# A new opening for a Fourier mixer with an ELU layer pair: the filter straight into SBUF, the first unit's layer products plain, the weight conversion rearranged

## The chip, the core and the metric

One core of a Trainium2 chip. The kernel is one program; its time is the device time of one execution in microseconds (us), the median of the runs shown. TensorE (PE) does the matrix products, VectorE (DVE) and ScalarE (ACT) the work on elements, GpSimd (POOL) mostly issues DMA transfers, SyncE (SP) issues nearly all others. Each engine works through its own instructions in their order.

## The reference

Two blocks, one after the other. The first filters along the sequence: a real Fourier transform over 3008 positions, a product with a complex filter, and the inverse transform. The second is a layer pair with ELU between.

```python
# x (8, 3008, 256) f32; filt_r, filt_i (1505, 256) f32
X = np.fft.rfft(x, axis=1)
Y = X * (filt_r + 1j * filt_i)[None]
y = np.fft.irfft(Y, n=3008, axis=1).astype(np.float32)
# y -> (24064, 256); w_in (256, 2048), w_out (2048, 256), both float64
h = y @ w_in
g = np.where(h > 0, h, np.exp(np.minimum(h, 0.0)) - 1.0)
out = (g @ w_out).astype(np.float32)
```

The layer weights arrive as 64-bit floats: 4.2 MB each. The kernel reads them as pairs of 32-bit words and makes 32-bit floats of them itself.

## The kernel before

**Fourier part.** 3008 = 47 x 64. The transform over 64 is a product with a table (`tf`/`ta`, PE, "psa"), the transform over 47 a second one (`gf`/`fb`), the filter a complex product, and the way back mirrors it (`gr`/`gi`, then `tn`/`tw`, "psn"). The 32 frequencies of the 64-transform are worked in eight groups of four.

The first batch (b = 0) has code of its own, inside the `boot` pool. `x_load_first` loads x in six chunks on SP; `a_first` multiplies each chunk as it comes and ACT lays the results into `zt` (two of the four `zt` tiles live in the not yet filled weights `w_in[3]`, `w_out[3]`); `t_first` transposes group g on PE; `b_first` does the 47-transform and `products`, four DVE instructions with the filter tile `ff[:, g]`; `bi_first` goes back and ACT copies the result into one of two `t3f` buffers; `y_write_first` writes it to DRAM scratch `yds[0]`. In the loop over g (L900) group g's forward part stands beside group g-2's way back. After the loop `y_read` brings the first unit's rows from scratch, seven products called `warm` keep PE at work meanwhile, and `n_unit(0, 0)` makes the layer's input y.

The filter goes two steps for the first batch: `f_arrange` (L785) writes it into DRAM scratch `fd` in the order of the groups, 28 transfers on POOL, half of them reading with a negative row step; `f_read_first` (L319) reads `ff` from `fd`, 16 transfers on POOL. `f_pairs` (L804) makes the layout `fp` that the other seven batches read, from `fd`, on SP, in quads 1 to 4.

**Weights.** Sixteen blocks k = 0 to 15; k = 4q + j, where q is the quarter of the hidden width and j = 0, 1 are halves of `w_in[q]`, j = 2, 3 of `w_out[q]`. `w_fetch` loads the 64-bit words (512 KB), `w_split` (DVE, two instructions) takes mantissa and exponent bits apart, `w_float` (ACT, four instructions) makes floats of the low word, of the mantissa, and of the exponent in two steps, `w_join` (DVE) puts the sign on, adds low word and mantissa, multiplies with the exponent's value into place. `w_sums` (DVE, four sums) makes the extra combinations that the layer's seven products need. Blocks 0 to 11 are done before the layer starts, 12 to 15 in quads 0 to 2.

**Layer part.** A unit is (b, m): 8 batches, six units of up to 512 tokens. Per unit and quarter q, one quad, items in the order b, m, q. Both layers are 2 x 2 blocks multiplied with seven products instead of eight (`up_steps`, `down_steps`; `COMBO` names the weight combination). Each product is two matmuls of 224 or 256 columns, four records in the trace: so 28 matmuls per quad. An up product lands in one of four PSUM banks "psM" (`bank`, `banks`, first in, first out); ACT copies some of them, DVE adds, ACT does the two steps of ELU (Relu, then Exp), DVE the last one (max) and the sums for the seven down products, which gather in the banks po0 to po3. The down products of a quad run beside the up products of the next one.

**Order.** Everything is in one hand-written order: `at(quad, place, fn)` puts a piece into a plan, and the loop at the end (L1022) takes up and down steps by turns ("UUDUDDU", then "DUUDUDD", or with another start where a quad is in `opens`) and calls the plan's pieces at places 2 and 3 (within the first string), 0 (between the strings) and 1 (after the second). Quad i = 4 is the first of unit (0, 1). In the first quads the next batch's first stage stands too: `x_unit` (DVE, two instructions each) for chunks 0, 1 at quad 2, 2, 3 at quad 3, 4, 5 at quad 4, and `a_unit`, which takes all four banks, after them; `z_write` and the first `z_read` go to SP, `b_unit` comes after quad 6.

SP's transfers use eight semaphores in turn, so each waits for the one eight before it.

Of the kernel before, what the change touches and what calls it, by code (L numbers as in the profile page):

```python
# [26 lines left out]
P = 128  # L27
# [14 lines left out]
def _make_tables():  # L42
# [78 lines left out]
    tw = np.ascontiguousarray(tn[:, 0:8].reshape(4, K2, 8, 2, 2, 32).transpose(1, 0, 2, 4, 3, 5)).reshape(P, 8, P)  # L121
# [12 lines left out]
def kernel(  # L134
# [48 lines left out]
    fd = fdp.tile([NG, 2, 48, 2, 2, D], FP32, name="fd")  # L183
# [105 lines left out]
    def t_first(g):  # L289

        t = t2s[0, g] = t4p.tile([P, 4, D], FP32, tag="t4", name="tf") if g % 4 > 1 else t2[:, g % 4]
        for j in range(2):
            i = j + 2 * (g % 2 if g < 4 else 0)
            ps = psO.tile([P, 2, 256], FP32, tag="po%d" % i, name="po%d" % i)
            for u in range(2):
                k = 4 * g + 2 * j + u
                for dh in range(2):
                    nc.tensor.transpose(ps[0:ROWS, u, ts(dh, P)], zt[k // 16][dh][:, ts(k % 16, ROWS)], eye)  # L298
            nc.scalar.activation(out=t[0:ROWS, 2 * j:2 * j + 2, :], in_=ps[0:ROWS], func=AXT.Copy)
# [19 lines left out]
    def f_read_first(g, t):  # L319
        for a, r in enumerate((LO, HI)):  # L320
            nc.gpsimd.dma_start(t[r].rearrange("p c u d -> p (c u d)"), fd[g, a].rearrange("q c u d -> q (c u d)"))
# [12 lines left out]
    def products(re, im, f, sr, si, p, q):  # L334

        nc.vector.tensor_tensor(out=sr, in0=re, in1=f[:, 0], op=ALU.mult)
        nc.vector.tensor_tensor(out=si, in0=re, in1=f[:, 1], op=ALU.mult)
        nc.vector.scalar_tensor_tensor(out=p, in0=im, scalar=-1.0, in1=f[:, 1], op0=ALU.mult, op1=ALU.mult)
        nc.vector.tensor_tensor(out=q, in0=im, in1=f[:, 0], op=ALU.mult)
# [144 lines left out]
    def y_read(b, m, *parts):  # L484
        t = t4s[b, m] = t4p.tile([P, 4, D], FP32, tag="t4", name="t4")
        for k in parts or (slice(0, K2),):
            if whole(b, m):
                r = slice(4 * k.start, 4 * k.stop)
                nc.sync.dma_start(t[r], yds[b].rearrange("k (p i) d -> (k p) i d", p=4)[r, 4 * m:4 * m + 4, :])
                continue  # L490
            for r in range(2):
                o = 64 * r
                nc.sync.dma_start(t[o + 2 * k.start:o + 2 * k.stop].rearrange("q i d -> q (i d)"),
                                  yds[b][k.start + r:k.stop:2].rearrange("k (p i) d -> k p (i d)", p=4)
                                  [:, :, 4 * m * D:4 * m * D + 4 * D])
# [5 lines left out]
    def n_whole(b, m):  # L501
# [10 lines left out]
        b11, b12, b21, b22 = rows  # L512
        t = yp.tile([P, 2, 256], FP32, tag="yb", name="yb")[:, :, 0:h]
# [38 lines left out]

    COMBO = {1: 0, 2: 2, 3: 6, 4: 3, 5: 4, 6: 5, 7: 1}
# [5 lines left out]
    def up_steps(b, m, q):  # L559

        h = half(m)
# [82 lines left out]
    def down_steps(b, m, q):  # L644
        h = half(m)
# [67 lines left out]
    def w_fetch(k, queue=nc.gpsimd):  # L713
        q, j = divmod(k, 4)

        if k in (3, 4, 14, 15):
            wd = t2[:, k % 11 - 3].rearrange("p u d -> p (u d)")
        elif k == 10:
            wd = t1p.tile([P, XC, D], FP32, tag="t1", name="wd").rearrange("p u d -> p (u d)")
        elif k in (6, 7, 8, 9):  # L720
            wd = xp.tile([P, 2, 2, D], FP32, tag="xc", name="wd").rearrange("p k u d -> p (k u d)")
        else:
            wd = fbufs[{5: 0, 11: 0, 12: 1, 13: 2}.get(k, k)].rearrange("p c u d -> p (c u d)")
# [14 lines left out]
    def w_split(k):  # L738
        m, e, f, l = wts[k] = wtmp[{9: 2, 10: 1, 11: 0, 12: 3, 13: 4, 15: 5}.get(k, k % 2)]
# [4 lines left out]
    def w_float(k, *parts):  # L744
        m, e, f, l = wts[k]
        ef = e.bitcast(FP32)
        steps = ((l, wds[k][:, :, 0], AXT.Identity, 2.0 ** -52, 0.0), (f, m, AXT.Identity, 2.0 ** -20, 1.0),
                 (ef, e, AXT.Relu, -8.0, edges[:, 0:1]), (e, ef, AXT.Relu, -1.0, edges[:, 1:2]))
        for i in parts or range(4):
            o, x, func, scale, bias = steps[i]  # L750
            nc.scalar.activation(out=o, in_=x, func=func, scale=scale, bias=bias)

    def w_join(k, parts=(0, 1)):
        q, j = divmod(k, 4)
        m, e, f, l = wts[k]
        if 0 in parts:
            nc.vector.scalar_tensor_tensor(out=e, in0=wds.pop(k)[:, :, 1], scalar=0x80000000, in1=e,
# [319 lines left out]
```

## Time and profile before

| what | us |
|---|---|
| median of 3 runs | 2560.32 (2559.58 to 2561.1) |
| profiled execution, its own time | 2561.57 |
| its span | 2559.8 |
| PE busy | 2519.9 |
| DVE busy | 2067.4 |
| ACT busy | 1543.9 |

The span runs from the first to the last instruction of the profiled execution. Three stretches of 20 us in the opening, from the view that sums each engine's busy time in a window (columns: window, its length, busy us and instructions of PE, its weight loads, DVE, ACT and POOL, the granted PE clock, the DMA engines' share, GB/s):

```profile
40.00:60.00 20.00, 19.01 (x144) 13.38 (x148) 15.52 (x31) 14.95 (x31) 9.56 (x18) 0.91 1.00 285
80.00:100.00 20.00, 15.73 (x74) 12.07 (x73) 16.70 (x36) 16.66 (x31) 0.00 (x0) 1.00 0.96 252
100.00:120.00 20.00, 18.33 (x104) 17.98 (x103) 18.81 (x36) 14.33 (x26) 0.00 (x0) 1.00 0.32 95
```

A matmul's record is drawn out while it waits, so a busy PE is not a PE at full speed: 74 records between 80 and 100 us, against 120 in 20 us further on. From some 160 us on PE is busy without a gap.

### The profile page before, as it was taken

How to read it: one execution, taken by the hardware profiler on the slowest of the kernel's cores; microseconds unless marked ns; L12 is line 12 of the kernel's file. 1: busy time of each engine (PE TensorE's matmuls, PEld its weight loads, DVE VectorE, ACT ScalarE, POOL GpSimd, SP SyncE). 2: the span in 40 equal slices, each digit the busy share in tenths (PEclk: the TensorE clock that was granted, in tenths of full speed). 3: DMA queues.
4: the chain of work that ended last, by engine and by line, in shares of the span. 5: the costliest groups of instructions: out<-in, count | busy, mean ns of one | idle time of the engine just before them, and what ended most of it. 6: DMA issues, size and time to landing. Idle time of an engine off the chain costs nothing.

```text
span 2559.8 us, 43989 instructions
## 1 busy us (share of the span) xinstructions
PE 2519.9 (98%) x16682; PEld 2162.6 (84%) x16682; DVE 2067.4 (81%) x3578; ACT 1543.9 (60%) x2715; POOL 159.5 (6%) x315
## 2 busy tenths in 40 slices
PE   6999999999999999999999999999999999999998
PEld 4788889888898888988889888888889888898887
DVE  6978887788878888688877888778897788876766
ACT  6766556655566555666566656566655655555554
POOL 5001000000000000000000000000100010000000
PEclk9999999999999999999999999999999999999999
DMA  9662213523233221433225231353213322110010
GB/s 282 183 186 67 59 44 78 131 63 71 48 99 98 69 66 40 127 81 74 51 51 143 66 77 36 77 123 80 66 38 84 87 63 63 38 44 18 20 27 17
DMA packets 229879, 200.56 MB, mean 78 GB/s; under 512 B 129398, under 2 KB 201990, under 8 KB 229668
## 3 DMA queue, kind: packets, MB, share of 16 engines
q1 hardware_dynamic: 214308, 166.86, 26.6%
q0 software_dynamic: 14000, 30.44, 4.2%
q8 instruction: 131, 2.15, 0.4%
q14 instruction: 80, 0.66, 0.1%
q10 hardware_dynamic: 1360, 0.46, 0.1%
HBM read 125.80 MB, written 78.12 MB: 80 GB/s over the span
## 4 chain that ended last, share of the span: by engine, by line
PE 96%; DMA 2%; DVE 1%; ACT 0%; issue 0%; SPq 0%; DVEq 0%; ACTq 0%
PE po L656 45%; PE phs L574 25%; PE phd L574 13%; PE pha L574 6%; PE psn L526 2%; PE psa L236 2%; PE pf L387 1%; PE pv L459 1%; DMA xc<-in_x_dram 1%; PE po L332 0%; DMA x<-in_x_dram 0%; PE po L298 0%; PE psr L332 0%; PE psa L279 0%; DVE g L582 0%
## 5 line engine op out<-in xcount | busy, mean ns | idle before, releaser
L656 PE MATMUL po<-g,wo 128*128 128x256 f32 (+1 forms) x5376 | 1317.7, 377 | 0.0
L656 PEld LDWEIGHTS po<-g,wo 128*128 128x128 f32 x5376 | 1010.7, 190 | 165.8 <-issue 49.6
L585 ACT ACTIVATE g<-phs 128x512 f32<-128x512 f32 (+1 forms) x576 | 338.8, 588 | 736.7 <-PE phs L574 735.3
L592 ACT ACTIVATE e<-e 128x512 f32<-128x512 f32 (+1 forms) x768 | 477.2, 621 | 24.4
L596 DVE SCALAR_TENSOR_TENSOR g<-e,g 128x512 f32<-128x512 f32 (+1 forms) x576 | 387.5, 673 | 13.7 <-ACT e L592 13.3
L582 DVE TENSOR_TENSOR g<-phd,g 128x512 f32<-128x512 f32 (+1 forms) x384 | 259.0, 674 | 165.1 <-ACT e L592 107.6
L574 PE MATMUL phs<-y,wi 128*128 128x256 f32 (+1 forms) x1536 | 387.6, 375 | 1.3 <-ACT y L509 1.3
L574 PE MATMUL phd<-y,wi 128*128 128x256 f32 (+1 forms) x1504 | 380.3, 375 | 0.0
L591 ACT ACTIVATE e<-g 128x512 f32<-128x512 f32 (+1 forms) x576 | 354.4, 615 | 34.3 <-DVE g L582 26.8
L574 PEld LDWEIGHTS phs<-y,wi 128*128 128x128 f32 x1536 | 291.4, 190 | 34.7 <-ACT y L509 1.5
L574 PEld LDWEIGHTS phd<-y,wi 128*128 128x128 f32 x1504 | 284.8, 190 | 35.1 <-DVE g L582 2.7
L596 DVE SCALAR_TENSOR_TENSOR g<-e,phs 128x512 f32<-128x512 f32 (+1 forms) x192 | 129.9, 677 | 115.2 <-ACT e L592 115.2
L574 PE MATMUL phs<-yt,wi 128*128 128x256 f32 (+1 forms) x768 | 193.9, 375 | 0.9 <-ACT g L585 0.9
L574 PE MATMUL phs<-yb,wi 128*128 128x256 f32 (+1 forms) x768 | 193.8, 375 | 0.6 <-ACT g L585 0.6
L574 PE MATMUL pha<-yb,wi 128*128 128x256 f32 (+1 forms) x736 | 185.9, 375 | 0.0
L591 ACT ACTIVATE e<-phs 128x512 f32<-128x512 f32 (+1 forms) x192 | 112.3, 585 | 111.9 <-PE phs L574 111.8
L582 DVE TENSOR_TENSOR g<-pha,g 128x512 f32<-128x512 f32 (+1 forms) x192 | 129.5, 674 | 44.8 <-PE pha L574 44.8
L574 PEld LDWEIGHTS phs<-yt,wi 128*128 128x128 f32 x768 | 145.7, 190 | 18.0 <-ACT g L585 1.5
L574 PEld LDWEIGHTS phs<-yb,wi 128*128 128x128 f32 x768 | 144.0, 190 | 19.3 <-ACT g L585 1.0
L326 POOL DMA_DIRECT2D fall<-fp x224 | 110.0, 499 | 721.9 <-DVE r L432 697.1
L574 PEld LDWEIGHTS pha<-yb,wi 128*128 128x128 f32 x736 | 139.8, 190 | 16.1
L633 DVE TENSOR_TENSOR g<-g,g 128x512 f32<-128x512 f32 (+1 forms) x192 | 130.7, 681 | 6.7
(166 smaller groups left out, 2063.3 us busy)
## 6 DMA issues: line engine op xcount, KB each, us to landing
yd<-t SPq DMA_DIRECT2D x127, 192.0 KB
t<-yd SPq DMA_DIRECT2D x92, 256.0 KB
z<-t SPq DMA_DIRECT2D x84, 256.0 KB
fall<-fp POOLq DMA_DIRECT2D x224, 96.0 KB, 2.9
t<-z SPq DMA_DIRECT2D x224, 96.0 KB
out_dram<-o SPq DMA_DIRECT2D x632, 32.0 KB
xc<-in_x_dram SPq DMA_DIRECT2D x84, 128.0 KB
xc<-in_x_dram SPq DMA_DIRECT2D x161, 64.0 KB
```

What stands on the lines that cost most here:

```text
L236: nc.tensor.matmul(p[o:o + 64, u, :], w[r, u, o:o + 64], src[r, u, :], start=True, stop=True)
L326: nc.gpsimd.dma_start(t[32 * a:32 * a + 24].rearrange("p c u d -> p (c u d)"), fp[g, a].rearrange("q c u d -> q (c u d)"))
L387: nc.tensor.matmul(pf[p][1][32 * a:32 * a + 32, js, :], fb[r, v, :], t2[r, js, a, :], start=True, stop=True, tile_position=(32 * p, 32 * a))
L526: nc.tensor.matmul(p[ts(c, 64), dh, ts(q, 64)], t[r, i - 4 * m, ds(dh * P + 64 * c, 64)], w[r, i - 4 * m, :], start=True, stop=True)
L574: nc.tensor.matmul(ps[:, a, 0:h], w_in[q][:, COMBO[n], a, :], y[n], start=start and a == 0, stop=True, skip_group_check=True)
L582: nc.vector.tensor_tensor(out=g[o], in0=i0, in1=i1, op=ALU.add)
L585: nc.scalar.activation(out=g[o], in_=i0, func=AXT.Copy)
L591: nc.scalar.activation(out=e, in_=src, func=AXT.Relu, scale=-1.0)
L592: nc.scalar.activation(out=e, in_=e, func=AXT.Exp, scale=-1.0)
L596: nc.vector.scalar_tensor_tensor(out=g[n], in0=es[n], scalar=1.0, in1=src, op0=ALU.subtract, op1=ALU.max)
L633: nc.vector.tensor_tensor(out=b12, in0=b22, in1=b12, op=ALU.subtract)
L656: nc.tensor.matmul(po[i][:, u, 0:h], w_out[q][:, COMBO[n], a, :], g[n][:, a, :], start=q == 0 and a == 0 and n in (1, 3, 6, 4), stop=True, ...
```

## The change

Five parts.

1. **Filter.** `f_arrange`, `fd` and the 16 reads are gone. `f_read_first(k, n)` loads rows k to k+n of the filter straight into `ff`, which has a new layout (real or imaginary, then 16 rows); once with 4 rows, once with 12. Per half and part: 24 partitions by one SP transfer; the mirrored rows, 16 partitions by SP and 7 by POOL. The SP ones stand behind x in the queue. The groups therefore hold other frequencies: two from the lower half, two from the upper (`t_first`, table `tw`), and later units read y's rows of the first batch by four transfers instead of two. `f_pairs` reads from the filter itself.
2. **First unit plain.** For (b, m) = (0, 0) each layer is eight products instead of seven (`plain_ups`, `plain_downs`), 32 matmuls per quad instead of 28. The DVE sums around them (adds, four sums after ELU, seven at the end) and the ACT copies between them go; four ELUs per quad stay.
3. **Conversion.** `w_float` has three ACT instructions instead of four; the mantissa's is now part of a DVE instruction in `w_join` that multiplies and adds. `w_float` writes the low word in place.
4. **When.** Blocks 0 to 3 before the last chunks of x are multiplied, one block in each of groups 3 to 8, block 10 begun after the loop; `w_join` of 10 to 15 and split and float of 11 to 15 in quads 0 to 2. No `w_sums` before quad 1; one to two of them at the ends or middles of quads 1 to 6. None of them on POOL.
5. **Queues.** Blocks 0 to 2 on POOL ahead of all else; all other blocks on SP: 3 behind chunk 3 of x, 4 to 8 behind the filter, 9 to 11 between y's writes, 12 to 15 behind y's read.

```diff
+    def f_read_first(k, n):
+        for c, src in enumerate((filt_r, filt_i)):
+            for a in range(2):
+                o, row, e = 64 * a, 16 * a + k, 1 if k == a == 0 else 0
+                nc.sync.dma_start(ff[o:o + 48:2, c, k:k + n].rearrange("q k d -> q (k d)"),
+                                  raw(src, row, [[64 * D, 24], [1, n * D]]))
+                for j, m, queue in ((0, 16, nc.sync), (16, 7, nc.gpsimd)):
+                    queue.dma_start(ff[o + 2 * j + 1:o + 2 * (j + m):2, c, k + e:k + n],
+                                    raw(src, 64 * (j + 1) - row - e, [[64 * D, m], [-D, n - e], [1, D]]))
...
     def f_pairs(c, u):
-        nc.sync.dma_start(dst[:, :, 0, :], src[:, 0:48:2, :])
+        nc.sync.dma_start(dst[:, :, 0, :], raw(src, u, [[2 * D, 2 * NG], [64 * D, 24], [1, D]]))
         g = 1 - u
-        nc.sync.dma_start(dst[g:, 1:24, 1, :], src[g:, 1:46:2, :])
+        nc.sync.dma_start(dst[g:, 1:24, 1, :].rearrange("g k d -> k g d"),
+                          raw(src, 64 - 2 * g - u, [[64 * D, 23], [-2 * D, 2 * NG - g], [1, D]]))
...
+    def plain_ups(b, m, q):
+        def step(i, j, k):
+            if k == 0:
+                held[i, j] = bank("php")
+            n, ps = held[i, j]
+            for a in range(2):
+                nc.tensor.matmul(ps[:, a, 0:h], w_in[q][:, 2 * k + i, a, :], rows[k][j],
+                                 start=k == a == 0, stop=True, skip_group_check=True)
+            if k == 1:
+                src = ps[:, :, 0:h]
+                e = ep.tile([P, 2, 256], FP32, tag="e", name="e")[:, :, 0:h]
+                nc.scalar.activation(out=e, in_=src, func=AXT.Relu, scale=-1.0)
+                nc.scalar.activation(out=e, in_=e, func=AXT.Exp, scale=-1.0)
+                nc.vector.scalar_tensor_tensor(out=g[i, j], in0=e, scalar=1.0, in1=src, op0=ALU.subtract, op1=ALU.max)
+                banks.append(held.pop((i, j))[0])
...
+    def w_float(k):
+        m, e = wts[k]
+        ef, l = e.bitcast(FP32), wds[k][:, :, 0]
+        steps = [(l.bitcast(FP32), l, AXT.Identity, 2.0 ** -52, 1.0),
+                 (ef, e, AXT.Relu, -8.0, edges[:, 0:1]), (e, ef, AXT.Relu, -1.0, edges[:, 1:2])]
...
+        nc.vector.scalar_tensor_tensor(out=f, in0=m, scalar=2.0 ** -20, in1=l, op0=ALU.mult, op1=ALU.add)
...
+                if 3 <= g < 9:
+                    if g > 3:
+                        w_join(g)
+                    w_split(g + 1)
+                    w_float(g + 1)
+                if 4 <= g < 7:
+                    w_fetch(g + 5)
...
+        for quad, place, fn, k in ((0, 2, w_join, 10), (0, 2, w_split, 11), (0, 2, w_float, 11),
+                                   (0, 0, w_join, 11), (0, 0, w_split, 12), (0, 0, w_float, 12),
+                                   (1, 2, w_join, 12), (1, 2, w_split, 13), (1, 2, w_float, 13),
+                                   (1, 0, w_join, 13), (1, 0, w_split, 14), (1, 0, w_float, 14), (1, 1, w_sums, 1),
+                                   (2, 2, w_join, 14), (2, 2, w_split, 15), (2, 2, w_float, 15), (2, 0, w_join, 15),
+                                   (2, 1, w_sums, 3), (2, 1, w_sums, 5), (3, 0, w_sums, 9), (3, 1, w_sums, 7),
+                                   (4, 1, w_sums, 13), (5, 1, w_sums, 11), (6, 1, w_sums, 15)):
```

More of the change, by code (lines that the diff above doesn't have):

```diff
@@ L772, in w_join, with w_sums @@
                 nc.vector.tensor_tensor(out=dst[:, i], in0=f[:, i], in1=e[:, i], op=ALU.mult)
-        if j % 2 == 1 and k < 7:
-            w_sums(k)
-    def w_sums(k, engine=nc.vector, parts=(0, 1, 2, 3)):
+    def w_sums(k, parts=(0, 1, 2, 3)):
         q, j = divmod(k, 4)
@@ L902 @@
                 if g < NG:
-                    b_first(g, ff[:, g], pqs[g % 2], back)
+                    b_first(g, [ff[:, c, 2 * g:2 * g + 2] for c in range(2)], pqs[g % 2], back)
                 else:
@@ L943 @@
         n_unit(0, 0)
-        n_sums(0, 0)
         PER = 24
```

242 lines of the change are left out of this document (111 added, 131 removed).

## The prediction

> **What bounds the kernel now.** I read the page first, then stretches of the opening, then the chain of waits, then TensorE, VectorE, ScalarE and the queues in order of time.
>
> ```profile
> span 2559.8 us, 43989 instructions
> PE 96%; DMA 2%; DVE 1%; ACT 0%; issue 0%; SPq 0%; DVEq 0%; ACTq 0%
> PE   6999999999999999999999999999999999999998
> ```
>
> TensorE (PE) ends the run with 96% of the chain, and only the first of the 40 slices (64 us each) shows it short of work. So the change counts in two ways: when TensorE reaches its unbroken run, and how much work it has. The chain and the order of time through the opening:
>
> ```profile
> 29.50 10.89 DMA x<-in_x_dram
> 40.53 3.63 PE psa L279 x16
> 49.39 0.69 DVE L336 TENSOR_TENSOR rq<-psr,ff 128x512 f32<-128x512 f32 x1 [3.71 <-PE psi L332]
> 77.63 0.59 ACT L365 ACTIVATE t<-po 128x512 f32<-128x512 f32 x1
> 84.71 2.02 PE L508 MATMUL psn<-tn,t 128*128 128x128 f32 x16 [1.45 <-DMA t<-yd]
> 88.01 1.02 PE L574 MATMUL phs<-y,wi 128*128 128x224 f32 x4 [1.28 <-ACT y L509]
> 136.37 1.02 PE L656 MATMUL po<-g,wo 128*128 128x224 f32 x4
> ```
>
> The last part of x lands at 40.4, the first filter product runs at 49.4, the last result of the eight frequency groups is copied at 78.2, the first layer product starts at 88.0, and the fifth quad at 136.4 (a quad is one quarter of the hidden width for one unit; from there on PE has no gap that matters). So the opening to the end of quad 3 is 136.4 us, in three stages: load (to 40), groups (49 to 78), first unit (88 to 136).
>
> ```profile
> 0.00:20.00 20.00, 3.89 (x17) 3.66 (x18) 14.00 (x26) 15.38 (x21) 11.92 (x26) 1.00 0.93 255
> 20.00:40.00 20.00, 12.11 (x64) 11.27 (x64) 9.15 (x20) 11.25 (x26) 8.72 (x16) 0.83 1.05 343
> ```
>
> The two columns at the end: DMA is busy throughout, at 255 and then 343 GB/s. The load stage is bound by bytes.
>
> **Load stage.** The copy of the filter into DRAM scratch (3.08 MB), the weights 4 to 6 and most of the filter no longer stand ahead of x. What must land up to x's end: x 3.08 MB, tables 1.57, weights 0 to 3 (4 x 512 KB) 2.10, the filter's 7-row parts that POOL issues early, 7/47 of 3.08 = 0.46; 7.2 MB. At the rates above: 5.1 MB by 20 us, then 2.1 MB / 343 GB/s = 6.1; x ends at 26, not 40.4. From x to the first product took 49.4 - 40.4 = 9.0, same instructions: 35. The rest of the filter and the small tables (2.9 MB, 8.6 us) land by 35 to 38; groups 0 and 1 need only the first 4 rows, group 2 starts at 40. The filter therefore costs nothing on this path; without that cover of 2 us, up to 5 us (bounds: 343 GB/s, and half that for 16-row and 24-row transfers, which no row shows filling the engines).
>
> **Group stage: VectorE becomes its bound.** Products cost 4 x 0.60 = 2.4 per group. A weight costs w_split 0.67 (76.91 to 77.58) and w_join 2.0:
>
> ```profile
> 100.31 0.68 DVE L757 SCALAR_TENSOR_TENSOR zq<-fall,zq 128x512 uint32<-128x512 uint32 x1
> 100.91 0.69 DVE L759 TENSOR_TENSOR zq<-zq 128x512 f32<-128x512 f32 x1
> 101.70 0.69 DVE L766 TENSOR_TENSOR wi<-zq 128x512 f32<-128x512 f32 x1
> 102.31 0.42 DVE L741 TENSOR_SCALAR t<-t 128x512 uint32<-128x512 uint32 x1
> ```
>
> (starts 100.31 to 102.31). The new fused multiply-add over integers isn't in the trace; nearest are L757's 0.60 between starts and 0.72 for the add with its wait. I take 0.72; the other end is worth under 1 us over the stage. ScalarE's float drops from four instructions to three; the one that writes in place is off the chain, since it waits for the DMA alone.
>
> Groups 0 to 2: 7.2. Group 3 with split 4: 3.1. Groups 4 to 7, each products, join, split: 4 x 5.07 = 20.3. Then no products hide ScalarE: two exponent steps 1.45, copy of group 6 1.07, join 8 and split 9 on VectorE meanwhile (30.6 + 1.4 + 2.0 + 0.7 = 34.7), exponents of 9 1.45, copy of group 7 1.07: 37.3. The result of group 0 is written behind weights 5 to 8 in SP's ring (2.25 MB with its table, about 8 us from 42, so 50), and group 2's copy into the same buffer waits for it from 46; ScalarE's float 5 slides, and join 5 by 0.8. End of stage: 35 + 37.3 + 0.8 = 73.1, against 78.2.
>
> From there to the first layer product was 88.0 - 78.2 = 9.8. Of it 1.7 was the copy of y waiting behind three conversions on ScalarE (its half was ready at 85.7, copied at 87.4); only conversion 10 is left there, under the 6.5 us of y's round trip. So 8.1, plus 0.8 for a colder PE, since its seven warming products now end 4 us before y comes: first layer product T = 82.0. **Gain so far 6.0.**
>
> **First unit: ScalarE and VectorE hand weights to and fro.** PE work: 32 + 24 products up to quad 4 at 0.755 (8 records take 1.51), 42.3; with 1.9 for the next unit's y and 2 x 1.9 for the next batch's first stage, 48.0. Before took 48.4 with 42.6 of work. Work alone would lose nothing. But before had only two floats (14, 15) left in it; after has five (11 to 15), six joins and five splits, written into one in-order queue with the ELUs:
>
> ELU's two steps 1.2, its VectorE max 0.55, join 2.0, split 0.67, the next float's exponents 1.45 (they need the split), hand-offs 0.15: 6.0 us before the next ELU. Those rows are these two, and L757 to L741 above:
>
> ```profile
> 92.83 0.57 ACT L591 ACTIVATE e<-g 128x448 f32<-128x448 f32 x1
> 93.43 0.58 ACT L592 ACTIVATE e<-e 128x448 f32<-128x448 f32 x1
> 111.97 1.47 ACT L751 ACTIVATE t<-t,edges 128x512 f32<-128x512 uint32 x2
> ```
>
> Quads 0 and 1 have two such cycles and two plain ELUs each, 2 x 6.0 + 2 x 1.2 = 14.4, while PE needs 6.0 and 12.1. A product's bank is free only after its max, and there are four. From T + 1.7: quad 0 to T + 16.1, quad 1 to T + 30.5, the copies of y to T + 31.7. PE waits about 3 us in quad 1, and 5 before quad 2. VectorE then: sums of weight 1 and of the next y 3.2 (T + 34.2), max, join 14, split 15 3.2, float 1.5, ELU 1.2 (T + 40.2), max, join 15, x_unit's four sums 0.55 + 2.0 + 2.65, two maxes 1.1: T + 46.5. Only then is the last of four banks free for a_unit, where PE has waited since T + 43. Its second half 1.0, quad 3's 16 products 12.1, the next a_unit 2.0: quad 4 starts at T + 61.6. Against 48.4: **13.2 lost.** The eighth down product in quad 4 adds 0.76. The weight sums that moved to quads 2 to 6 (1.6 each) lie under 12 to 15 us of PE in quads where VectorE has 3 to 5 us idle (139 to 160), and the first unit's output loses its seven adds; if not hidden, 1 to 2 us. y's four reads for two, on SP, lie 13 us ahead of need.
>
> Sum: -6.0 + 13.2 + 0.8 = +8.0. Profiled 2559.8 (2561.6 with what lies around the span, 1.3 above the median 2560.3): 2567.8 span, 2568.3 as a median; I say 2569 for a PE that cools in the 5 us wait (40.53 above: 16 records took 3.63 after 2.28 idle, against 2.02 after 1.41 at 24.98).
>
> **Rivals.**
> 1. *The waits in the first unit are hidden* (faster). If PE never waits for a bank, quad 4 starts at 82.0 + 48.0 = 130.0: -6.4 + 0.8, about 2555. For it: ScalarE has 8.9 us of work per quad, VectorE 8, under PE's 12.1. Against: the order above is fixed. It decides when the cycle is below (12.1 - 2.4) / 2 = 4.8 us. Chance 0.11. Half the waits: 2562, within 0.2% (5 us, about what a measurement here can tell). With milder openings 0.19.
> 2. *The opening gains nothing*: one queue doesn't draw 300 GB/s, or VectorE waits for the filter in each group. T = 88, 2575. For: all of the ten first filter transfers are under 100 KB. Against: SP issues eight before it waits for the first. 0.12.
> 3. *The pair filter goes through one engine.* f_pairs now writes odd rows as 23 rows of 15 or 16 KB-pieces; before as 15 or 16 rows of 23.
>
> ```profile
> DMA packets 337, 0.34 MB, mean 331 GB/s; under 512 B 1, under 2 KB 337, under 8 KB 337
> q1 hardware_dynamic: 337, 0.34, 99.5%
> ```
>
> This is 1.04 us of such a transfer in before: 16.6 engine-us for 337 packets, 49 ns each. If 23 rows sat on one engine, 345 and 368 packets would hold it 17 and 18 us, four times in quads 0 to 5, with SP's ring behind them. The last pair would land near T + 101, the next batch's z behind it, read at T + 104, where b_unit wants it at T + 102 (before it had 13 us of slack): +2, 2571; if each packet took 70 ns, z writes and y's read slip too: 2580 to 2600. Chance that it shows in the time: 0.18. The Trainium skill ("DMA: Bandwidth & Descriptors", "Why a DMA increments its semaphore by 16 and not by 1") gives a transfer as many engines as the largest number up to 16 that divides the slowest dimension of both sides: 15 or 16 for before's, which agrees with the engines full above, and one for 23 rows. By that rule this rival holds, at 2571.
>
> **How the numbers follow.** Forecast 0.40, its own range 2565 to 2574 (T 79 to 85, waits 10 to 15). Rival 3 0.18, rival 2 0.12, between 0.19, rival 1 0.11. Faster 0.11, same 0.19, slower 0.70. Range 2558 to 2584: it drops rival 1 and the jammed end of rival 3.
>
> **What would show it.** x's last psa near 26 to 30; first product near 35; first layer product near 82; in quads 0 to 2 ScalarE idle on VectorE's split, PE idle in three pieces of 2 to 5 us, quad 4 near 144; no f_pairs transfer holding SP. Wrong if quad 4 starts before 134, or if TensorE is broken after 160.

## The result, and the profile after

The changed kernel takes 2603.1 us (median of 4, 2598.86 to 2605.34) against 2560.71 of the kernel before beside it (2559.58 to 2561.97): ratio 1.0163, 95% interval 1.015 to 1.0175, so slower by 1.6%. The forecast was 2569, its range 2558 to 2584: too fast by 34. The profiled execution took 2598.86, the fastest of the four, with a span of 2597.1; the forecast's span was 2567.8, so 29.3 us are to be explained.

The page of the profile after, the lines that answer to the first fence of the prediction:

```profile
span 2597.1 us, 43965 instructions
PE 93%; DVE 2%; DMA 2%; SPq 1%; ACT 1%; issue 1%; DVEq 0%; ACTq 0%
PE   6798999999999999999999999999999999999998
```

PE still ends the run, but its share of the chain fell from 96 to 93%, SP's queue went from 0 to 1%, and two more of the 40 slices are thin. The loss lies in the first 260 us. The load stage, by windows (columns: window, length, busy us and instructions of PE, its loads, DVE, ACT and POOL, PE clock, DMA share, GB/s), then the order of time through the opening on PE, DVE and ACT:

```profile
0.00:20.00 20.00, 5.51 (x32) 5.18 (x32) 9.97 (x16) 13.29 (x19) 8.48 (x20) 1.00 0.94 228
20.00:40.00 20.00, 16.31 (x120) 14.93 (x124) 5.77 (x12) 11.48 (x28) 0.00 (x0) 0.83 0.89 210
```

```profile
31.76 2.02 PE L279 MATMUL psa<-t,x 128*128 128x128 f32 x16 [0.22 <-DMA x<-in_x_dram]
39.01 0.69 DVE L345 TENSOR_TENSOR rq<-psr,ff 128x512 f32<-128x512 f32 x1 [6.17 <-PE psi L340]
50.13 0.69 DVE L346 TENSOR_TENSOR rq<-psr,ff 128x512 f32<-128x512 f32 x1 [4.62 <-DMA ff<-in_filt_i_dram]
51.94 0.68 DVE L345 TENSOR_TENSOR rq<-psr,ff 128x512 f32<-128x512 f32 x1
81.41 0.59 ACT L374 ACTIVATE t<-po 128x512 f32<-128x512 f32 x1
88.13 3.24 PE L518 MATMUL psn<-tn,t 128*128 128x128 f32 x16 [2.29 <-DMA t<-yd]
91.16 1.21 PE L585 MATMUL php<-y,wi 128*128 128x224 f32 x3
153.63 1.02 PE L608 MATMUL po<-g,wo 128*128 128x224 f32 x4
```

x lands at 31.7 (before 40.4), the first filter product runs at 39.0 (49.4), group 2 waits for the filter until 50.1, group 3 begins at 51.9, the last group is copied at 82.0 (78.2), the layer begins at 91.2 (88.0), quad 4 at 153.6 (136.4). x came 8.7 us sooner and the layer 3.2 later. In the first unit PE has three clear gaps, each behind DVE's max of an ELU (L592):

```profile
101.14 1.02 PE L585 MATMUL php<-y,wi 128*128 128x224 f32 x4 [1.02 <-DVE g L592]
107.01 1.78 PE L585 MATMUL php<-y,wi 128*128 128x224 f32 x8 [1.82 <-DVE g L592]
120.77 3.36 PE L585 MATMUL php<-y,wi 128*128 128x224 f32 x8 [4.64 <-DVE g L592]
```

And behind quad 4 stands what the forecast left to a rival. Three of the four long stops of SP's queue, a window of the first of them, and the waits for z behind the third (from 150.9) and the last, with a window that shows PE's clock at 0.66. z is the first stage's results, written to scratch and read back.

```profile
108.89 12.29 SPq L870 DMA_DIRECT2D fp<-nil_t  x1
123.39 14.14 SPq L870 DMA_DIRECT2D fp<-nil_t  x1
179.67 12.37 SPq L870 DMA_DIRECT2D fp<-nil_t  x1
```

```profile
109.00:121.00 12.00, 6.61 (x40) 6.23 (x40) 6.42 (x13) 6.36 (x11) 0.00 (x0) 0.93 0.16 52
```

```profile
172.47 1.09 ACT L240 ACTIVATE t<-psa 128x512 f32<-128x512 f32 x2 [3.83 <-DMA z<-t]
174.10 2.08 PE L648 MATMUL phs<-yt,wi 128*128 128x256 f32 x4 [2.57 <-ACT g L659]
204.42 1.83 PE L396 MATMUL pf<-t,pairs 24*32 24x256 f32 x4 [6.41 <-DMA t<-z]
206.87 4.76 PE L396 MATMUL pf<-t,pairs 24*32 24x256 f32 x36 [0.62 <-DMA t<-z]
211.56 2.08 PE L732 MATMUL po<-g,wo 128*128 128x256 f32 x4
```

```profile
200.00:220.00 20.00, 14.93 (x71) 8.80 (x72) 8.37 (x15) 4.26 (x9) 1.95 (x4) 0.66 0.66 151
```

L870 is the 15 KB of zeros that `f_pairs` issues directly behind its 23-row transfer; the stop not shown, third in time, runs from 150.9 for 11.5 us. While SP stands there, the DMA engines are 0.16 busy; in the finer view from 110 to 120 us the rate soon falls to a flat 25 GB/s, 1 KB each 41 ns, and from 113 to 120 us the share is 0.07, about one engine of 16. 345 such packets are 14.1 us.

The first product of the second batch's way back ("pv") comes at 252.4 against 214.8; from there on the two kernels run alike. So the 37.6 us between the kernels at pv (37.3 in the whole span) are 3.2 to the layer, 14.1 in the first unit (62.5 for 48.4) and 20.3 from quad 4 to pv.

### The profile page after: what moved, and what is told of

It reads as the page before. It is cut to its first block, busy times and chain, and to the rows that moved or that the text cites. A ratio compares the mean times of both kernels' runs of the same rounds, so it can differ in the third digit from the quotient of the medians.

```text
span 2597.1 us, 43965 instructions
## 1 busy us (share of the span) xinstructions
PE 2543.7 (98%) x16714; PEld 2175.7 (84%) x16714; DVE 2049.0 (79%) x3543; ACT 1529.6 (59%) x2687; POOL 135.4 (5%) x272
## 4 chain that ended last, share of the span: by engine, by line
PE 93%; DVE 2%; DMA 2%; SPq 1%; ACT 1%; issue 1%; DVEq 0%; ACTq 0%
PE po L732 43%; PE phs L648 24%; PE phd L648 12%; PE pha L648 6%; PE psn L539 2%; PE pf L396 1%; PE psa L236 1%; PE pv L468 1%; DMA t<-tf_t 1%; PE php L585 1%; PE po L608 1%; SPq L781 0%; DMA z<-t 0%; DMA t<-yd 0%; DMA ff<-in_filt_i_dram 0%
## 5 line engine op out<-in xcount | busy, mean ns | idle before, releaser
L732 PE MATMUL po<-g,wo 128*128 128x256 f32 (+1 forms) x5264 | 1294.3, 378 | 0.0
L732 PEld LDWEIGHTS po<-g,wo 128*128 128x128 f32 x5264 | 990.8, 190 | 165.8 <-issue 49.0
L659 ACT ACTIVATE g<-phs 128x512 f32<-128x512 f32 (+1 forms) x564 | 332.3, 589 | 735.8 <-PE phs L648 734.4
L666 ACT ACTIVATE e<-e 128x512 f32<-128x512 f32 (+1 forms) x752 | 468.0, 622 | 23.9
L670 DVE SCALAR_TENSOR_TENSOR g<-e,g 128x512 f32<-128x512 f32 (+1 forms) x564 | 379.8, 673 | 13.4 <-ACT e L666 13.1
L656 DVE TENSOR_TENSOR g<-phd,g 128x512 f32<-128x512 f32 (+1 forms) x376 | 253.7, 675 | 166.7 <-ACT e L666 108.3
L648 PE MATMUL phs<-y,wi 128*128 128x256 f32 (+1 forms) x1504 | 380.8, 376 | 0.0
L665 ACT ACTIVATE e<-g 128x512 f32<-128x512 f32 (+1 forms) x564 | 347.5, 616 | 32.0 <-DVE g L656 27.2
L648 PEld LDWEIGHTS phs<-y,wi 128*128 128x128 f32 x1504 | 286.2, 190 | 33.3
L648 PEld LDWEIGHTS phs<-yt,wi 128*128 128x128 f32 x752 | 143.2, 191 | 19.5 <-ACT g L659 3.0
## 6 DMA issues: line engine op xcount, KB each, us to landing
yd<-t SPq DMA_DIRECT2D x127, 192.0 KB
```

The source lines that it names most:

```text
L648: nc.tensor.matmul(ps[:, a, 0:h], w_in[q][:, COMBO[n], a, :], y[n], start=start and a == 0, stop=True, skip_group_check=True)
L656: nc.vector.tensor_tensor(out=g[o], in0=i0, in1=i1, op=ALU.add)
L659: nc.scalar.activation(out=g[o], in_=i0, func=AXT.Copy)
L665: nc.scalar.activation(out=e, in_=src, func=AXT.Relu, scale=-1.0)
L666: nc.scalar.activation(out=e, in_=e, func=AXT.Exp, scale=-1.0)
L670: nc.vector.scalar_tensor_tensor(out=g[n], in0=es[n], scalar=1.0, in1=src, op0=ALU.subtract, op1=ALU.max)
```

## The experiments

Each took 3 or 5 rounds beside the kernel before, whose median was 2560.6 to 2563.1. The moments below are those of the profiled executions. x's end is that of its last "psa" product on PE; it lies between 33.8 and 39.3 in executions whose opening is the same up to there, so the columns count from one moment to the next.

| kernel | us | ratio (95%) | x's end | layer, behind x | 3rd a_unit, behind layer | pv, behind it |
|---|---|---|---|---|---|---|
| before | 2560.7 | | 44.1 | 43.9 | 59.9 | 66.9 |
| after | 2603.1 | 1.0163 (1.015-1.0175) | 33.8 | 57.4 | 74.7 | 86.5 |
| e1_pairs16 | 2584.1 | 1.0084 (1.0067-1.0101) | 38.7 | 57.7 | 75.5 | 68.2 |
| e2_before23 | 2592.3 | 1.0119 (1.0104-1.0134) | 42.7 | 46.3 | 61.6 | 93.6 |
| e3_split_first | 2571.0 | 1.004 (1.0025-1.0055) | 39.3 | 56.8 | 64.1 | 68.3 |
| e4_filter_once | 2599.2 | 1.015 (1.0135-1.0165) | 37.5 | 72.1 | 75.0 | 68.3 |
| e5_before_newconv | 2559.8 | 0.9994 (0.9985-1.0003) | 41.8 | 42.1 | 60.0 | 67.0 |
| e6_pitch61 | 2571.7 | 1.0044 (1.003-1.0058) | 34.5 | 58.1 | 64.3 | 68.2 |
| e7_convert_early | 2572.9 | 1.0041 (1.0027-1.0054) | 38.2 | 57.1 | 62.7 | 68.2 |
| e9_two_queues | 2583.2 | 1.0084 (1.007-1.0098) | 46.2 | 58.0 | 64.7 | 68.2 |
| e10_first_piece_only | 2570.9 | 1.0037 (1.0022-1.0051) | 35.5 | 58.5 | 65.0 | 68.2 |
| e11_weights_between | 2576.7 | 1.0063 (1.0048-1.0078) | 37.1 | 58.0 | 64.0 | 68.2 |
| e12_rows_upward | 2574.3 | 1.0055 (1.004-1.007) | 35.7 | 57.8 | 65.1 | 68.2 |
| e13_copies_first | 2571.5 | 1.0035 (1.0021-1.0049) | 38.5 | 52.9 | 67.0 | 68.2 |
| e14_convert_in_gap | 2568.1 | 1.0028 (1.0017-1.004) | 39.0 | 52.5 | 64.6 | 68.2 |
| e15_first_unit_28 | 2574.1 | 1.0053 (1.0039-1.0067) | 34.5 | 50.5 | 75.3 | 67.0 |

### SP's stops: e1 and e2

e1, the kernel after with the 23 odd rows in two transfers:

```diff
-        nc.sync.dma_start(dst[g:, 1:24, 1, :].rearrange("g k d -> k g d"),
-                          raw(src, 64 - 2 * g - u, [[64 * D, 23], [-2 * D, 2 * NG - g], [1, D]]))
+        for j, m in ((0, 16), (16, 7)):
+            nc.sync.dma_start(dst[g:, 1 + j:1 + j + m, 1, :].rearrange("g k d -> k g d"),
+                              raw(src, 64 * (j + 1) - 2 * g - u, [[64 * D, m], [-2 * D, 2 * NG - g], [1, D]]))
```

> The changed kernel with one edit: the odd rows of the pair filter go as 16 and 7 rows instead of 23. Theory A (a transfer of 23 rows sits on one DMA engine, SP is held 12 to 14 us behind each of the four, and the next batch's z is late): SP shows no hold over 2 us there, quads 4 to 8 lose nothing, 2603 falls by some 20 us to 2583 (2579 to 2587). Rival B (the loss after quad 4 comes from VectorE's moved sums and conversions, the transfers only stand beside it): at or above 2598.

2584.1: 19.0 less, with one transfer more in each `f_pairs`. pv comes 68.2 behind the third a_unit instead of 86.5, and no issue of `f_pairs` holds SP for more than 1.2 us. PE's only gap from 150 to 245 us is one of 1.1, and the `pf` products, 7.1 us from first to last in after, take 1.6. e2 gives the kernel before the same shape:

```diff
-        nc.sync.dma_start(dst[g:, 1:24, 1, :], src[g:, 1:46:2, :])
+        nc.sync.dma_start(dst[g:, 1:24, 1, :].rearrange("g k d -> k g d"),
+                          src[g:, 1:46:2, :].rearrange("g k d -> k g d"))
```

> The kernel before with one edit: the odd rows of the pair filter, still read from the scratch copy, go as 23 rows of 15 or 16 instead of 15 or 16 rows of 23; same bytes. Theory A: SP is held 12 to 14 us four times from 100 us on, and PE waits for z or y's rows behind it: slower by 5 to 20 us, 2566 to 2581. Rival B: 2560 to 2562.

30.9 us slower (2592.3 against 2561.4), more than expected; the same four rows are there:

```profile
101.84 13.08 SPq L811 DMA_DIRECT2D fp<-nil_t  x1
117.27 14.43 SPq L811 DMA_DIRECT2D fp<-nil_t  x1
```

So it is the transfer's outermost 23, and what else has changed is not needed for it. PE waits longer here than in after: 11.2 us behind ACT at 167.4 and 7.2 for z at 198.5.

### The first unit: e3 and e7

e3 is e1 with another order in quads 0 to 2: split and float of the next block ahead of the join of the last.

```diff
-        for quad, place, fn, k in ((0, 2, w_join, 10), (0, 2, w_split, 11), (0, 2, w_float, 11),
+        for quad, place, fn, k in ((0, 2, w_split, 11), (0, 2, w_float, 11), (0, 2, w_join, 10),
...
```

> e1_pairs16 with one more edit: in quads 0 to 2 w_split and w_float of the next weight block stand ahead of w_join of the last one, so that ScalarE's float no longer waits for the join. Theory C (ScalarE and VectorE hand a block to and fro in cycles of 6 us, five times, and PE waits for banks): the cycle falls to 4 us, the first unit from first layer product to quad 4 from 62.5 to 52 to 55 us, 7 to 10 us faster than e1_pairs16. Rival D (the first unit is long because of its 56 products, the next batch's first stage and the four banks): within 2 us of e1_pairs16.

13.1 us less than e1, more than the 7 to 10 expected; the third a_unit comes 64.1 behind the layer for 75.5. Of e1's gaps of 1.0, 1.8 and 4.7 us on PE, one of 1.1 is left. The hand-over between DVE and ACT was most of the loss (before has 59.9), by its order alone: no work was taken away. e7 takes blocks 10 and 11 out of the unit as well:

```diff
+            w_split(10); w_float(10); w_join(9); w_split(11); w_float(11); w_join(10); w_join(11)
-            w_join(9); w_split(10); w_float(10)
...
```

> e3_split_first with the weight blocks 10 and 11 converted before the first layer product, where VectorE and ScalarE stand idle for some 9 us while y goes to memory and back, and only blocks 12 to 15 inside quads 0 to 2. VectorE's work there is two joins of 2.0 and a split of 0.8 more, which fits. Theory C (ping-pong of conversion and layer in the first unit is what is left of its loss): the first x block's transforms of quad 1, which come 33.8 us behind the first layer product in e3 and 32.9 in before, come 31 to 33 behind it, the layer starts within 1 us of e3's 96, and the time is 2567 to 2570 (e3 2571.0). Rival D: it only moves: the layer starts 2 or more us later, or the unit keeps its length because PE's banks were not waiting for these blocks; time within 1.5 us of 2571.

1.4 us less in the unit (62.7), and 2572.9 (2567.89 to 2573.6): not to be told from e3.

### The opening: the filter

e4 is e1 with the filter in one piece, `for k, n in ((0, 16),)` in place of `((0, 4), (4, 12))`.

> e1_pairs16 with one more edit: the filter's 16 rows in one go, 10 SP transfers instead of 18. Theory E (SP's 0.65 to 0.9 us per issue bounds the filter's loading): first filter product later by 2 to 5 us, but group 2 no longer waits 4.6 us in the middle of its products, and the layer starts 2 to 4 us earlier: 2 to 4 us faster than e1_pairs16. Rival F (the engines bound it: 24 rows on few engines, short packets): between 1 us faster and 3 us slower.

Both theories missed: 15.1 us more. The layer comes 72.1 behind x. With no early piece, PE has nothing to do for 5.8 us, and its clock falls:

```profile
51.55 1.97 PE L340 MATMUL psr<-tf,once 48*64 48x512 f32 x2 [5.83 <-DVE rq L346]
```

```profile
46.00:48.00 2.00, 0.00 (x0) 0.00 (x0) 0.00 (x0) 0.47 (x1) 0.00 (x0) 1.00 0.91 151
56.00:58.00 2.00, 2.00 (x15) 1.22 (x11) 0.69 (x1) 0.00 (x0) 0.00 (x0) 0.50 0.21 78
66.00:68.00 2.00, 2.00 (x13) 0.39 (x6) 0.24 (x1) 0.17 (x1) 0.00 (x0) 0.50 0.00 0
```

From 51.6 to 70 us PE's records leave no gap, at half its clock; its 48x512 products take 1.06 us instead of 0.59. The filter was there at 50.8, hardly another time than in after (50.1), though SP was through with its issues 2 us sooner. That speaks against SP's issues as what sets the landing.

Then what does? From 42 to 50 us all engines are busy at some 200 GB/s, and at 390 once the weights follow. e6 and e12 try two causes, e6 with `61 * D` for `64 * D` as the filter's row distance, e12 with `[D, n - e]` for `[-D, n - e]`, starting at the other end.

> e3_split_first with the first batch's filter read at rows 61 KB apart instead of 64 KB: the same transfers, sizes and queues, but other rows of the filter, so the first batch is multiplied by wrong filter values. In the opening of the kernel after the change the cores' 16 engines are all busy from 42 to 50 us and move only 200 GB/s, and 390 GB/s as soon as the weights follow at 50; the filter's 12 KB packets take 863 ns each, where a 4 KB packet of the weights takes 160 to 170. Theory P: it is the 64 KB between the rows that all engines read at once. Then at 61 KB the 12 KB packets take 500 to 650 ns, the stretch from 42 to 50 shows 280 GB/s or more, group 2's product waits 2 to 4 us less for its data, and the time is 2567 to 2570 (e3 2571.0). Rival Q: short runs into few partitions are slow whatever the pitch: 12 KB packets stay above 800 ns, 190 to 215 GB/s, time within 2 us of 2571.

> e3_split_first with the odd filter rows of the opening read upward through memory instead of downward: the same rows and bytes in the reverse order, so that each partition gets them in the wrong order and the first batch is multiplied by wrong values. Downward each row is a packet of 1 KB; upward 12 rows are one run. Theory O (the 200 GB/s from 42 to 50 us come from the 1 KB packets, of which some 2450 lie between 24 and 62 us): the 1 KB packets fall by about 1000, the stretch shows 260 GB/s or more, group 2's data lands 2 or more us earlier, time 2567 to 2569 against 2571. Rival P: the 12 KB packets go on taking 800 ns and more and the stretch stays below 220 GB/s: time 2570 to 2573, and the cause lies elsewhere.

Neither. In e6 the 12 KB packets take 872 ns on average (840 in e3); the windows:

```profile
44.00:48.00 4.00, 4.00 (x31) 2.45 (x29) 1.26 (x2) 1.27 (x3) 0.00 (x0) 1.00 1.05 203
52.00:56.00 4.00, 3.69 (x27) 1.30 (x30) 4.00 (x8) 1.89 (x4) 0.00 (x0) 1.00 1.03 384
```

In e12 the 1 KB packets between 24 and 62 us fall from 2446 to 1454, and the engines still move 186 GB/s from 44 to 48. Why they are this slow stays open. One difference was not tried: each of these transfers writes 24, 16 or 7 of the 128 partitions, where a weight's writes all of them. e9 sends the imaginary half by POOL:

```diff
-        for c, src in enumerate((filt_r, filt_i)):
+        for c, (src, first) in enumerate(((filt_r, nc.sync), (filt_i, nc.gpsimd))):
```

> e3_split_first with the imaginary filter's transfers of the opening issued by the idle GpSimd queue instead of SP, 9 of 18. Theory I (the opening's second limit is SP's issues, 0.62 to 0.90 us each and one after the other, while the DMA engines are busy for 0.40 to 0.70 of the time from 32 to 40 us): the share rises to 0.8 or more there, SP is through with the filter 6 us earlier, group 2's data is there 2 to 4 us earlier, and the time is 2567 to 2569. Rival J (the engines' rate is the limit, or GpSimd makes its descriptors more slowly than SP issues): the last imaginary rows land no earlier, time 2570 to 2576.

12.2 us more than e3, for a reason that neither theory had: POOL doesn't stand behind x, so its transfers run beside x's until 33 us, and PE waits for x:

```profile
31.95 3.75 PE L279 MATMUL psa<-t,xc 128*128 128x128 f32 x16 [5.73 <-DMA xc<-in_x_dram]
```

x's end slips from 39.3 to 46.2, the rest keeps its length (58.0). Last, e10 leaves the second piece out (`for k, n in ((0, 4),)`, and `2 * (g % 2)` for `2 * g` in the groups' slices).

> e3_split_first without the second piece of the first batch's filter (rows 4 to 15 of each part: 9 of the 18 transfers on SP, about 2.1 of 2.9 MB): groups 2 to 7 are multiplied by the rows of groups 0 and 1, so they leave out their own filter. Theory K (the forecast's failed term: the filter is no free passenger, groups 2 and on wait for its second piece, which lands around 50 us): the first products start where they do in e3, groups follow one another without the stop of 2 to 5 us, the weights 4 to 8 come 9 us earlier, and the first layer product comes 6 to 10 us earlier, 86 to 90 against 96; time 2562 to 2566 against 2571. Rival L (VectorE's conversions or x's arrival set the group stage anyway): at most 2 us earlier, 2569 or more.

2570.9, where e3 has 2571.0. DVE's products of groups 2 and 3 in e10:

```profile
46.49 0.69 DVE L345 TENSOR_TENSOR rq<-psr,ff 128x512 f32<-128x512 f32 x1 [0.93 <-PE po L340]
52.05 0.69 DVE L345 TENSOR_TENSOR rq<-psr,ff 128x512 f32<-128x512 f32 x1 [2.71 <-PE po L340]
```

The wait for the filter is gone and one for PE stands in its place. Group 3 begins 11.4 us behind the first product in e10 (52.05 - 40.68) and 12.9 in after (51.94 - 39.01): of after's 4.6 us of waiting for the filter 1.5 counted. In e3, which has the filter's second piece and waits 2.3 us for it, it is 11.4 too: there the filter cost nothing.

### The opening: the conversions

e11 fetches blocks 4 and 5 between the filter's pieces and starts the group stage's conversions two groups sooner.

```diff
+            f_read_first(0, 4)
+            for k in (4, 5):
+                w_fetch(k)
+            f_read_first(4, 12)
...
-                if 3 <= g < 9:
+                if 1 <= g < 7:
```

> e3_split_first with weight blocks 4 and 5 fetched between the two pieces of the filter, and the conversions of the group stage begun two groups earlier, so that VectorE has them to do while the second piece lands (it is idle for some 5 of the 6 us from 44 to 50). Theory M (the group stage is VectorE's sum of products and conversions, and every idle us of it counts): the two blocks' 1 MB delays the second piece by about 3 us at 390 GB/s, two conversions of 2.7 to 3 us leave the end of the stage, the first layer product comes 2 to 4 us earlier, time 2567 to 2569 against 2571. Rival N: the weights wait for x's buffers and hold SP's queue, or the later second piece takes back what the conversions give: time 2571 to 2575.

Slower by 5.7 in the median; the layer 58.0 behind x. Group 2 waits 5.0 us for the filter, until 54.6: what DVE won sooner the filter took back. Why the median is 5.7 higher the profiles don't show: e11's execution (2573.9) is its fastest, e3's (2575.1) its slowest.

e13 and e14 start from a stop at the end of the stage. In after, ACT:

```profile
75.31 1.48 ACT L829 ACTIVATE we<-we,edges 128x512 f32<-128x512 uint32 x2 [2.04 <-DVE we L820]
79.55 1.48 ACT L829 ACTIVATE we<-we,edges 128x512 f32<-128x512 uint32 x2 [1.24 <-DVE we L820]
80.93 0.58 ACT L373 ACTIVATE t<-po 128x512 f32<-128x512 f32 x1
```

PE has ended the last group's products at 76.5; the copy stands in ACT's order behind block 9's exponents, and these behind DVE's split of block 9.

```diff
-                if 3 <= g < 9:
+                if 3 <= g < 6:
...
-            w_join(9); w_split(10); w_float(10)
+            for k in (7, 8, 9):
+                w_split(k); w_float(k); w_join(k - 1)
...
```

> e3_split_first with the conversions of weight blocks 7, 8 and 9 taken out of the group stage: blocks 4 to 6 are converted beside groups 3 to 5 as before, 7 and 8 behind the last group's copies while y goes to memory and back, and one more block than in e3 falls into quads 0 to 2. In the kernel after the change PE ends the last group's products at 76.5, but ScalarE copies them out only at 80.9 to 82.0, because ScalarE, in order, first waits for VectorE's split of block 9 and converts it; the same 4.4 us lie there in e10, which had no filter to wait for and gained nothing. Theory R (the opening's end is set by the conversions ahead of the copies on ScalarE, and by VectorE's 5.05 us per group where PE alone would take about 4): the last copy comes 40 to 43 us behind the end of x's last transforms (47.3 in e3, 48.2 in after), the first layer product 5 to 7 us earlier than in e3, time 2563 to 2567 against 2571. Rival S (the conversions only move: y's copies wait for them on ScalarE instead, or the third block in quad 0 draws the first unit out): the layer starts at most 2 us earlier or the unit is 3 or more longer, time 2569 to 2573.

The first half of theory R holds: the last copy ends 38.7 behind x's end (77.2 - 38.5; e3 47.3). But only 3.9 of these 8.6 us reach the layer (52.9 behind x for 56.8), and the unit takes 2.9 back:

```profile
77.22 0.36 ACTq L381 DMA_DIRECT2D yd<-t  x1
87.89 3.75 PE L518 MATMUL psn<-tn,t 128*128 128x128 f32 x16 [5.12 <-DMA t<-yd]
91.44 4.89 PE L585 MATMUL php<-y,wi 128*128 128x224 f32 x24
```

From the last copy to the layer it is now 14.2 us, for 9.5 in e3. y's read is issued 5.8 us behind the last write (77.22 to 83.05), for 0.6 in e3. The writes of the last groups come closer together, with DMA at 0.97 from 76 to 80 us; that this is the reason was not tried. Time as e3. e14 puts blocks 9 and 10 into that gap too, by `(7, 8, 9, 10)` and a `w_join(10)` behind it, with e3's list for the quads less `w_join` of 10:

> e13_copies_first with blocks 9 and 10 also converted before the first layer product, where VectorE stood idle in e13 from 84.4 to 94.6 us, so that quads 0 to 2 hold only blocks 11 to 15. In e13 the first layer product came 52.9 us behind the end of x's last transforms (e3 56.8) and the first unit's third x block 67.0 behind the layer (e3 64.1). Theory R (each conversion taken out of the unit gives back its part, and the gap has room): the layer stays 52 to 54 behind x, the third block comes 62.5 to 64 behind it, time 2567 to 2569 against 2571.5. Rival S: ScalarE's floats of the two blocks (4.2 us) push y's copies back by 2 us or more, and the time stays at 2570 to 2573.

2568.1, the best of the changed kernel's line: the layer 52.5 behind x, the unit 64.6, a little over what was expected. It is still 0.28% above before. e15 is e14 with the first unit in 28 matmuls (`plain` always false, weight and y sums put back):

> e14_convert_in_gap with the first unit's layer products made in 28 matmuls by sums of weights and of y, as in the kernel before: the sums of blocks 1 and 3 behind their conversion, those of 5 and 7 in the gap before the layer, the others in quads 0 to 3, y's five sums ahead of the first product. Theory U (what is left of the unit's loss is the 32 matmuls against 28 and one more ELU per quad on ScalarE): the third x block comes 1 to 3 us sooner behind the layer than in e14, the layer starts within 2 us of e14's, time 1 to 3 us below e14. Rival V (VectorE's sums, 1.7 us a block in quads 0 to 3 and y's sums before the first product, cost what the four matmuls save): time within 1 us of e14 or above.

6.0 us more than e14: rival V and worse. The layer begins 50.5 behind x, but its next product waits 3.4 us for y's sums, which stand on DVE behind the sums of blocks 5 and 7, and the unit is 10.7 longer. With these conversions in the gap the plain products are the better choice; another order of the sums wasn't tried.

### The conversion alone: e5

The kernel before with the new conversion and nothing else:

```diff
-        steps = ((l, wds[k][:, :, 0], AXT.Identity, 2.0 ** -52, 0.0), (f, m, AXT.Identity, 2.0 ** -20, 1.0),
+        steps = ((l.bitcast(FP32), l, AXT.Identity, 2.0 ** -52, 1.0), None,
...
-            nc.vector.tensor_tensor(out=f, in0=f, in1=l, op=ALU.add)
+            nc.vector.scalar_tensor_tensor(out=m.bitcast(FP32), in0=m, scalar=2.0 ** -20, in1=wd[:, :, 0].bitcast(FP32),
+                                           op0=ALU.mult, op1=ALU.add)
```

> The kernel before with one part of the change alone: a weight block's mantissa is no longer turned into a float by ScalarE; the join multiplies and adds in one VectorE instruction instead. In before the first layer product is held by y's copy, which waits for twelve ScalarE conversions that run back to back from 78.7 to 87.1 us; three of them (0.57 to 0.63 each, 1.8 us together) go. Theory G: y's copy starts up to 1.7 earlier, first layer product at 86.3 to 87.0 (before 88.0), time 2559 to 2560.5 against 2561 of the kernel before. Rival H: y's data or VectorE's joins end last there anyway, first layer product within 0.4 of 88.0. Neither lets it be slower by more than 1 us: the join's second instruction takes 0.68 in either form.

2559.8 against 2560.9, ratio 0.9994 (0.9985 to 1.0003): the lowest median of all, but not to be told from no change. In its profile the layer begins 8.4 us behind the last copy (83.91 - 75.5) instead of 9.8, which is theory G's size; of the other 2.7 us by which its layer is sooner, 2.3 come from an x that ended sooner.

## Why the prediction was wrong, step by step

**The step that failed is rival 3**, "the pair filter goes through one engine", priced at +2 with a chance of 0.18 and left out of the sum. It cost 19.0 us (after to e1), over half of the 34. Its mechanism was stated, with four transfers of 345 and 368 packets, "with SP's ring behind them", and so was its time: the last one was to end near T + 101 with T the layer's start, and SP came free at 192.0, T + 100.9. The packets weren't slower than priced but faster, 41 ns for 49. What failed is the price of what stands behind SP. The sum by which it got +2 has one item, the read of z, 3 us after SP came free. That z's writes and y's read slip too was named, at 2580 to 2600, but only for packets of 70 ns, and the range left it out. The record has three losses from quad 4 to pv:

- 4.5 us at 174. z's earlier writes are issued at 167.9, behind the stop from 150.9. ACT waits 3.8 us for them and PE 2.6 for ACT, and from 174 to 178 PE has a clock of 0.57.
- 11.9 us at z. It is written when SP is free (192.2 to 195.4), its read is issued at 200.6 and lands for PE at 204.4, T + 113.3, where T + 102 was wanted. PE has nothing to do for 6.4 us. From 204.4 to 212 its clock is then 0.50, while the rest of z still lands: the `pf` products take 7.1 us, where before takes 1.6.
- 3.1 us behind it: 1.7 at a clock of 0.81 (212 to 220), and 1.5 around a wait for y at 233.0.

With the 0.8 of the eighth down product these are the 20.3. Of them 10.7 are waits that the profile names; most of the other 8.8 is PE at work at a low clock behind such a wait. The forecast had terms for a cooling PE ahead of the layer and in the first unit, of under 1 us each, and none here. In e1 the waits and the low clock are gone together.

The Trainium skill ("DMA: Bandwidth & Descriptors", "Why a DMA increments its semaphore by 16 and not by 1") had the rule: one engine for 23 rows, 16 for 16 rows. e1 and e2 agree with it in both directions; it deserved the larger chance. What made the price is that the issuing queue stands still meanwhile.

The rival is not all of the error: without it (e1) the time is 2584.1, at the upper end of the range. Most of the rest lies in the opening, where T is 9.2 late.

**Load stage: its size was off.** "x ends at 26": 31.7. The bytes were nearly right, 7.6 MB moved by then for 7.2. The rate wasn't: 228 GB/s up to 20 us and 249 to 268 from there to 32, where I took 255 and 343 from the kernel before. (The 210 of the second window above is low because little moves from 32 to 38, when x is there.) The rest, 7.3 us from there to the first product, was near the 9.0 assumed. Product at 39.0 for 35: 4.0 lost.

**"The filter therefore costs nothing on this path"**: it costs 1.5 in after and nothing in e3. But the cover named for it was wrong. I had groups 0 to 2 at DVE's pace, 7.2 us; PE's transforms set them at 11.4 (e10), and with the filter's 1.5 group 3 begins 12.9 behind the first product: 5.7 lost. The 11.4 stood in the profile of the kernel before, where group 3's first product comes 11.4 behind the 49.39 of the first:

```profile
60.74 0.69 DVE L336 TENSOR_TENSOR rq<-psr,ff 128x512 f32<-128x512 f32 x1 [0.71 <-PE po L332]
```

The line of after alone, 4.6 us of waiting for the filter, would have named the wrong cause.

**Group stage from group 3 on: right.** 30.1 us to the last copy for 30.9 forecast, with DVE's 5.05 per group for 5.07 and ACT's copies behind the conversions. e13 shows what that order costs: 8.6 us at the last copy, 3.9 at the layer.

**y's round trip: right**, 9.2 for 8.9. So T is 91.2 for 82.0: 4.0 + 5.7 - 0.8 + 0.3.

**First unit: right.** 62.5 for 61.6, by the mechanism that was given, DVE and ACT handing weights to and fro (e3). Another order of the same work saves most of it (e3).

**Sum**: 9.2 + 0.9 + 19.5 (20.3 behind quad 4, less the 0.8 forecast for the eighth down product) = 29.6 of the 29.3. The median lies another 4.2 above this profiled execution; the profiles of the kernels with the same opening, where x ends up to 5 us later, suggest that it is the opening that varies, but no run shows what makes it.

Rival 1 fell: the waits in the unit weren't hidden. Rival 2 (the opening gains nothing) named the right end, T at 88 or later. Of its two causes the lower rate is the load stage's 4.0; DVE's wait for the filter is 1.5 at most (e10).

What ate x's 10 us (x's last product ended at 33.8 for 44.1)? The layer comes 57.4 behind x instead of 43.9, and the rows say where these 13.5 lie: 1.5 up to group 3, 12.6 from group 3 to the last copy (30.1 for 17.5 in before), -0.6 from there to the layer. After's stretch holds the conversions of six blocks; in before 8 of the 12 blocks had been begun while x was still loading, in after only 4. With three of the six taken out the stretch is 20.6 us (e13; 30.8 in e3), but y's trip then takes 4.7 back. The forecast had this stretch right; the one ahead of it, up to group 3, it had too short.

## What to carry to other kernels

Look at the outermost dimension of every transfer that is rewritten, and price a single-engine transfer by everything behind it on its queue, round trips through memory included, not by its own bytes. To each wait of PE that this makes, add what its products lose at a low clock behind it (here most of 8.8 us, on waits of 10.7). When a load gets shorter, list the work that ran beneath it and say where it runs now; where it then passes between two in-order engines, start the next item's first half ahead of the last item's second half (e3: 13 us by order alone). A wait that the profile names is worth only its lead over the next one: take it away in an experiment before repairing it. And read a stage's pace off the kernel before, where it is already there.

## What the runs showed of the hardware that was not expected

- A transfer of 345 or 368 packets of 1 KB on one engine holds the next issue of its queue for 11.5 to 14.4 us (eight times, in after and e2), not just its own landing.
- PE's clock fell to half after 5.8 us without work and stayed there for 18 us in which its records leave no gap (e4, 51.6 to 70 us). The Trainium skill ("TensorE: Matmul & The Clock Gate", "What's actually happening") has it fall after an idle window of about 3.4 us, which agrees (1.00 until 48 us, 0.50 from 50), and rise after one busy window of the same length, which these 18 us do not. They are mostly products over 48 rows into 64 columns. In after, products of these shapes are at 0.50 from 62 to 64 us, behind a gap of only 1.5, and at full clock again from 66: so the shape alone is not why it stayed low in e4, and the cause stays open.
- Behind a wait of 6.4 us, PE's clock was 0.50 for 7.6 us and 0.81 for the next 8 (after, 204.4 to 220); what PE loses there is not in the wait's own length.
- With all 16 engines busy, the filter's rows came at about 200 GB/s and the weights right behind them at 390. Neither the 64 KB between rows (e6) nor the 1 KB packets (e12) made the difference.
